# Output weights of two decode-attention problems in larger transfers: wo as 16 rows per partition

## The chip, the cores and the metric

The kernel runs on one core of one Trainium2 chip. The metric is the device time of one execution in microseconds (us). The times below are medians of several executions; the profile is of one execution.

## What is computed

Two independent problems, A and B, of the same shape are computed and their outputs are concatenated. Each is one step of decoding with a sliding window: 2 sequences, 1 query position, 32 query heads on 16 key and value heads, head size 128, a window of the last 4096 of 16384 cached positions, model width 576, all in bf16.

```
W = 4096; rep = 2
q = (x @ wq).reshape(B, Sq, Hq, Dh).transpose(0, 2, 1, 3)
k = repeat(k_cache[:, :, Sk - W:, :], rep, axis=1)
v = repeat(v_cache[:, :, Sk - W:, :], rep, axis=1)
p = softmax(einsum("bhqd,bhkd->bhqk", q, k) * Dh ** -0.5)
o = einsum("bhqk,bhkd->bhqd", p, v)
out = o.transpose(0, 2, 1, 3).reshape(B, Sq, Hq * Dh) @ wo      # wo: 4096 x 576
return concatenate([out_A, out_B], axis=-1)
```

## The kernel before

**Steps.** The work is cut into 16 steps, `ND` of them, 8 for A and 8 for B. A step is one slab of keys (4 MB: 4 pairs of sequence and key head, with 32 rows of each, 32 KB a partition) and the slab of values that belongs to it. Two steps make a group `G` of 8 query heads; there are 8 groups (`NG`), 4 in each problem (`GPP`). The slabs stream through a ring of 4 slots in SBUF (`ring`), all issued from the SP queue in one fixed order, `stream`: the two wq, then K0, K1, V0, K2, V1 and so on to K13, V12, K14, K15, V13, V14, V15. A slab's transfer waits until the slab four places before it has been read. V15, the last, comes in two pieces of 3 MB and 1 MB.

**One step.** For step `s` the vector engine (DVE) transposes the K slab in four parts (`do_X`, L494), and TensorE (PE) multiplies each with the spread-out queries `zq` (`do_S`, L519 and L170, into `st`). One step later come the maximum (`do_max`, L529), its transposition (`do_nm`, `do_nm2`, L542, L547), the exponential on ACT (`do_exp`, L564), the transposition of the result on DVE (`do_pC`, L572), and at the step's end the product with V (`do_PV`, L610, into `acc`), copied out by ACT (L622).

**One group.** GpSimd reduces the copied result (L629, L632, L637), `do_comb` turns it (L650), `do_norm` divides by the sums of the softmax (L674) and spreads the heads over 16 column positions (L683, `om`, with `maskD`). `do_redist` is two small matmuls with `maskS` (L710) that move the elements so that partition `p` holds what belongs to the rows of wo that lie on it; ACT copies this to `Rsb` (L730). `do_proj` then makes 8 pairs of matmuls, 512 and 64 columns wide, of `Rsb` with 8 rows of wo per partition (L757 and L170, into `ot` and a bank of `tb`). The sum over a problem's groups stays in `ot` for the 512 columns; the 64 are added up on DVE in `o_rest` (L773, L776). `do_E` finishes a problem.

**Order.** Each engine executes its instructions in the order in which this program adds them. A step's loop adds them over four parts `u`; the combine, norm and redistribute of group `G` stand in step `2G + 3`, and its projection at the end of that step, after the last `do_S` and ahead of `do_PV`:

```python
            do_S(s, NU - 1)
            if D2 >= 0 and D2 % 2 == 1 and s < ND - 1:
                do_proj(D2)
                if D2 == SPP - 1:
                    do_E(0)
```

with `D2 = s - 2`. So groups 0 to 5 are projected in steps 3, 5, 7, 9, 11 and 13. The add of the 64 columns is DVE's next instruction after `pC` and stands ahead of the next step's first transpose. Group 6 is projected in the tail after the last step, ahead of the two PV of V15; group 7, the last, in another form: its first step by a redistribution over 4 rows, its second by heads, from four last pieces of wo (L277 and L262) that are loaded behind V15.

**wo before.** `wob` has two buffers of 8 rows per partition. Group `G`'s 1152 KB of wo are one transfer (`issue_wo`, L275), ahead of K2, K4, K6, K8, K10, K12 and K14 in the stream; from group 2 on it waits for the projection of group `G - 2`.

Of the kernel before, what the change touches and what calls it, by code (L numbers as in the profile page):

```python
# [59 lines left out]
def build_kernel(nc, probs, out, cfg=None):  # L60
# [38 lines left out]
    PIECES = [(0, 96), (96, 128)]  # L99
    HEADS = [(0, 1), (2,), (3,)]  # L100
# [4 lines left out]

    es = ExitStack()
    with es:
# [3 lines left out]
        wqr = sb("wqr", [128, NPROB, HH], BF16)  # L111
        wob = sb("wob", [128, 2, 8, NOUT], BF16)
        xT = sb("xT", [128, NXC, NPROB, 128], BF16)
        maskP = sb("maskP", [128, 2], BF16)
        x_dup = sb("x_dup", [NPROB * Bb, DREM, 2], BF16)
        x_sb = sb("x_sb", [NPROB * Bb, D], BF16)
        ident_b = sb("ident_b", [128, 128], BF16)
        zq = sb("zq", [128, 4, NZQ, ZW], BF16)
        qrow = sb("qrow", [128, 1024], BF16)
        qtr = sb("qtr", [128, 1024], BF16)  # L120
# [5 lines left out]
        ones_b = sb("ones_b", [128, 128], BF16)  # L126
# [9 lines left out]
        oTg = sb("oTg", [128, 2, 16], BF16)  # L136
        om = sb("om", [128, 2, 256], BF16)
        Rsb = sb("Rsb", [128, 2, Bb, 8], BF16)
        maskS = sb("maskS", [128, 8], BF16)
        maskA = sb("maskA", [128, 4], BF16)  # L140
# [3 lines left out]
        mask4S = sb("mask4S", [128, 4], BF16)  # L144
# [3 lines left out]
        maskJ = sb("maskJ", [128, 4], BF16)  # L148
        ident_r = sb("ident_r", [128, 32], BF16)
        out_sb = sb("out_sb", [Bb, NPROB, NOUT], BF16)  # L150
# [57 lines left out]
        for G in range(NG):  # L208
            if not by_group(G):
                continue  # L210
            s_ = 2 * G + 2
            w_at.setdefault(("K", s_) if s_ < ND else ("V", s_ - LS), []).append(G)
# [11 lines left out]
        def issue_slab(n):  # L224
# [9 lines left out]
            if n == len(stream) - 1:  # L234
                for n_, (ja, jb) in enumerate(PIECES):
                    def fq(e, n_=n_, ja=ja, jb=jb):
                        return e.dma_start(ring[:, r, ja * 128:jb * 128], src[:, :, ja * 128:jb * 128]).then_inc(piece_sem[n_], 16)  # L237
                    pieces.append(dma_op("sp", piece_sem[n_], 1, fq, deps, "%s%d_q%d" % (kind, D_, n_)))
                issue_wo(NG - 1)
                return  # L240
# [16 lines left out]
        def issue_last(woP, pc, r0, deps):  # L257
            for n_, hs in enumerate(HEADS):
                def f(e, n_=n_, hs=hs):
                    t, r = divmod(hs[0], 2)  # L260
                    row = t * HH + r0 + 256 + 128 * r
                    return e.dma_start(wob[:, pc, 4 + hs[0]:4 + hs[0] + len(hs), :],  # L262
                                       woP[row:row + 128 * len(hs), :].rearrange("(h d) n -> d h n", d=128)).then_inc(wl_sem[n_], 16)
                wo_last.append(dma_op("sp", wl_sem[n_], 1, f, deps, "wl%d" % n_))

        def issue_wo(G):
            woP = probs[G // GPP][4]
            pc = G % 2
            r0 = (G % GPP) * 512
            deps = [proj[2 * (G - 2) + 1]] if G >= 2 else []  # L270

            def f(e):
                if by_group(G):
                    src = woP.rearrange("(t r) n -> t r n", t=2)[:, r0:r0 + 512, :].rearrange("t (p s) n -> p t (s n)", s=8)
                    return e.dma_start(wob[:, pc, :, :].rearrange("p s n -> p (s n)"), src).then_inc(wo_sem[pc], 16)  # L275
                src = woP.rearrange("(t r) n -> t r n", t=2)[:, r0:r0 + 256, :].rearrange("t (p s) n -> p t (s n)", s=4)
                last = e.dma_start(wob[:, pc, 0:4, :].rearrange("p s n -> p (s n)"), src).then_inc(wo_sem[pc], 16)  # L277
                return last
            wo_dma[G] = dma_op("sp", wo_sem[pc], 1, f, deps, "wo%d" % G)
            if not by_group(G):  # L280
                issue_last(woP, pc, r0, deps)

        def issue_until(n_needed):
            while nxt[0] <= n_needed:
                for G in w_at.pop(stream[nxt[0]], []):
                    issue_wo(G)
# [43 lines left out]
        def init_small():  # L330
# [5 lines left out]
                maskS[:], ident_b[:].rearrange("d (a s) -> d s a", s=8), AX.X, ALU.max), [p_ident_b], "maskS")  # L336
            init["mask4D"] = S.add("dve", lambda e: e.tensor_reduce(
# [325 lines left out]
        def do_norm(D_):  # L663
            G, sl = D_ // 2, D_ % 2
            n, bank = comb_at[D_]
            deps = [comb[D_], chain[(G, "rsb")]]
            if by_group(G):
                if G >= 2:
                    deps.append(spread[G - 2])

                def f_nm(e):
                    last = None
                    for l_ in range(2):
                        last = e.tensor_tensor(  # L674
                            oTg[:, G % 2, :].rearrange("d (b l r t) -> d l b t r", b=Bb, l=2, r=2)[:, l_],
# [4 lines left out]
                deps = [norm[D_], init["maskD"]]  # L680
                if G >= 2:
                    deps.append(redist[G - 2])
                spread[G] = S.add("dve", lambda e: e.tensor_tensor(  # L683
                    om[:, G % 2, :].rearrange("d (h k t) -> d h k t", h=8, t=2),
                    oTg[:, G % 2, :].rearrange("d (h t) -> d h t", t=2).unsqueeze(2).broadcast_to([128, 8, 16, 2]),
                    maskD[:].unsqueeze(1).unsqueeze(3).broadcast_to([128, 8, 16, 2]), ALU.mult), deps, "spread%d" % G)
                return
            dst = oTn[:, :, :].rearrange("d (t r) b -> d b t r", t=2) if sl else \
                oTg[:, G % 2, 0:8].rearrange("d (b r t) -> d b t r", b=Bb, r=2)
            if sl == 0:  # L690
                deps.append(spread[G - 2])
# [3 lines left out]
            if sl == 0:  # L695
                spread[G] = S.add("dve", lambda e: e.tensor_tensor(
                    om[:, G % 2, :].rearrange("d (h k t) -> d h k t", h=4, t=2),
                    oTg[:, G % 2, 0:8].rearrange("d (h t) -> d h t", t=2).unsqueeze(2).broadcast_to([128, 4, 32, 2]),
                    mask4D[:].unsqueeze(1).unsqueeze(3).broadcast_to([128, 4, 32, 2]), ALU.mult),
                    [norm[D_], init["mask4D"], redist[G - 2]], "spread%d" % G)  # L700
# [3 lines left out]
        def do_redist(G, idle=0):  # L704
            NS = 8 if by_group(G) else 4

            def fn(e, bank):
                last = None
                for b in range(Bb):
                    last = e.matmul(bank[:, NS * b:NS * b + NS], om[:, G % 2, 128 * b:128 * b + 128],  # L710
                                    maskS[:, :] if by_group(G) else mask4S[:, :], start=True, stop=True)
                return last
            last = [None]

            def fn_(e, bank):
                last[0] = fn(e, bank)
                return last[0]
            n, bank, op = tb_job(fn_, "redist%d" % G, [spread[G], init["maskS"], init["mask4S"]])
            if idle:
# [5 lines left out]
                S.add("pe", f_idle, [chain[(ND - 1, "exp")], init["maskB"]] + fin_ops, "idle%d" % G)  # L725
            redist[G] = op
            deps = [op, wo_dma[G]] if by_group(G) else [op]
            if G >= 2:
                deps.append(proj[2 * (G - 2) + 1])
            r_ev[G] = S.add("act", lambda e: e.activation(  # L730
                Rsb[:, G % 2, :, 0:NS], bank[:, 0:NS * Bb].rearrange("d (b s) -> d b s", b=Bb), ACTF.Copy), deps, "rev%d" % G)
            tb_consumer[n] = r_ev[G]
# [6 lines left out]
        def do_proj(D_):  # L739
            G = D_ // 2  # L740
            P = G // GPP
            pc = G % 2
            new = G % GPP == 0
            if by_group(G):
                parts = [([(Rsb[:, pc, :, s_], s_) for s_ in range(8)], [r_ev[G]], new, True, True)]
            elif D_ < ND - 1:
                parts = [([(Rsb[:, pc, :, s_], s_) for s_ in range(4)], [r_ev[G], wo_dma[G]] + fin_ops, False, False, False)]
# [3 lines left out]
            for lhs, deps, start, rstart, rstop in parts:  # L751
                def f(e, rest, lhs=lhs, start=start, rstart=rstart, rstop=rstop):
                    last = None
                    for n_, (l_, s_) in enumerate(lhs):
                        begin, end = n_ == 0, n_ == len(lhs) - 1
                        if by_group(G):
                            first = e.matmul(OT[0:Bb, 0:NB0], l_, wob[:, pc, s_, 0:NB0], start=start and begin, stop=end, skip_group_check=True)  # L757
                            last = matmul_again(e, first, rest[0:Bb, 0:NB1], wob[:, pc, s_, NB0:NOUT], rstart and begin, rstop and end)
                        else:
                            for half in range(2):  # L760
                                last = e.matmul(fin(half), l_, wob[:, pc, s_, half * NH:(half + 1) * NH],
# [28 lines left out]
        def do_E(P):  # L790
            G = (P + 1) * GPP - 1
            if G == NG - 1:
                e_ops[(P, 0)] = S.add("act", lambda e: e.activation(out_sb[:, P, 0:NH], fin(0), ACTF.Copy), [proj[2 * G + 1]], "Elo%d" % P)
                e_ops[(P, 1)] = S.add("dve", lambda e: e.tensor_copy(out_sb[:, P, NH:NOUT], fin(1)), [proj[2 * G + 1]], "Ehi%d" % P)
# [3 lines left out]
                out_sb[:, P, NB0:NOUT], o_rest[:, :], bank[0:Bb, 0:NB1], ALU.add), [proj[2 * G + 1], rest_add[G - 1]], "Ehi%d" % P)  # L798
            e_ops[(P, 0)] = S.add("act", lambda e: e.activation(out_sb[:, P, 0:NB0], OT[0:Bb, 0:NB0], ACTF.Copy), [proj[2 * G + 1]], "Elo%d" % P)

        def do_out(P, c0, c1, eng, deps):
            dma_op(eng, out_sem, 1, lambda e: e.dma_start(
                out[:, 0, P * NOUT + c0:P * NOUT + c1], out_sb[:, P, c0:c1]).then_inc(out_sem, 16), deps, "out%d_%d" % (P, c0))
# [13 lines left out]

        for s in range(ND):
            D2 = s - 2
            c = s - 1  # L820
            for u in range(NU):
# [21 lines left out]
                if D2 >= 0 and D2 % 2 == 1 and s < ND - 1:  # L843
# [3 lines left out]
                    elif u == 3:  # L847
                        do_redist(D2 // 2)
            do_S(s, NU - 1)
            if D2 >= 0 and D2 % 2 == 1 and s < ND - 1:  # L850
                do_proj(D2)
                if D2 == SPP - 1:
# [23 lines left out]
        do_redist(D_ // 2)  # L876
# [7 lines left out]
        do_redist(D_ // 2, 3)  # L884
# [107 lines left out]
```

## Time and profile before

| | |
|---|---|
| median of 3 executions | 363.21 us (363.21 to 363.26) |
| profiled execution | 363.24 us |
| its span, first to last instruction | 362.0 us |
| mean granted TensorE clock | 0.859 |
| moved by DMA | 153.27 MB, 423 GB/s over the span |
| busy: PE, DVE, ACT, GpSimd | 227.9, 202.0, 68.7, 35.4 us |
| DVE transposes of K (L494) | 64, mean 2285 ns, 145.4 us |
| chain that ended last | DMA 71%, DVE 15%, PE 9%, ACT 3% |
| transfers of wo by group (L275) | 7 of 1152 KB |

The rows of the timeline give the start and the duration in us, the engine, the line in the program, the operation, output and inputs with their shapes, a count, and in brackets how long the engine had been idle before and which instruction ended that. PEld is the loading of weights into TensorE, PE the matmuls themselves. In the view of waits the columns are the waiting engine and line, what released it, the sum of the waits in us, their number and the longest.

### The profile page before, as it was taken

To read this page: it belongs to the slowest core of one execution; us is meant where nothing else is said; L and a number is where in the kernel's file an instruction comes from. 1 tells how busy PE (TensorE), PEld (TensorE's weight loads), DVE (VectorE), ACT (ScalarE), POOL (GpSimd) and SP (SyncE) were. 2 spreads that over 40 slices of the span, in tenths; PEclk is the share of its full clock that TensorE was granted. 3 is DMA by queue.
4 is the path that set the end of the run, shared out by engine and by line. 5 is a ranking of instruction groups with operands and counts; after the bars stand their busy time and mean duration, and the time that the engine had idled before them with its cause. 6 is when DMAs were issued, how large, how long until landed. Compare 5 with 4: busy or idle time off the path is not lost.

```text
span 362.0 us, 2758 instructions
## 1 busy us (share of the span) xinstructions
PE 227.9 (63%) x1326; PEld 58.5 (16%) x953; DVE 202.0 (56%) x176; ACT 68.7 (19%) x153; POOL 35.4 (10%) x55
## 2 busy tenths in 40 slices
PE   0399195576966647384874727775672749657775
PEld 0010021112221202111221201111120112211121
DVE  3113599483818466291936648092844829179831
ACT  1036503020300303020110203102020203002131
POOL 1000000003100040004000040001300040110020
PEclk9999589787696969889688978869897896969999
DMA  8999999999999999999999999999999999999996
GB/s 348 420 449 406 453 389 446 438 431 432 439 415 445 424 427 440 420 442 427 405 455 427 431 433 424 435 435 427 426 434 431 438 422 431 435 427 442 418 421 251
DMA packets 7067, 153.27 MB, mean 423 GB/s; under 512 B 776, under 2 KB 1296, under 8 KB 1680
## 3 DMA queue, kind: packets, MB, share of 16 engines
q1 hardware_dynamic: 7052, 153.10, 98.8%
q8 instruction: 9, 0.15, 0.2%
q14 instruction: 2, 0.02, 0.0%
q10 hardware_dynamic: 4, 0.00, 0.0%
HBM read 153.10 MB, written 0.00 MB: 423 GB/s over the span
## 4 chain that ended last, share of the span: by engine, by line
DMA 71%; DVE 15%; PE 9%; ACT 3%; SPq 1%; issue 0%
DMA ring<-in_B_k_cache_dram 34%; DMA ring<-in_A_k_cache_dram 26%; DVE xt L494 13%; DMA wob<-in_B_wo_dram 8%; PE st L170 4%; PE st L519 4%; DMA x_sb<-in_B_x_dram 3%; ACT qrow L444 1%; DVE qtr L454 1%; ACT qk L462 1%; PE st L429 1%; DVE nM L542 1%; ACT qrow L449 1%; PE tb L532 0%; SPq L237 0%
## 5 line engine op out<-in xcount | busy, mean ns | idle before, releaser
L494 DVE STREAM_TRANSPOSE xt<-ring 128x2048 f32<-128x2048 f32 x64 | 145.4, 2285 | 76.0 <-DMA ring<-in_B_k_cache_dram 39.2
L519 PE MATMUL st<-xt,zq 128*128 128x512 bf16 x256 | 116.7, 456 | 111.1 <-DVE xt L494 84.8
L170 PE MATMUL st<-xt,zq 128*128 128x512 bf16 x256 | 115.5, 451 | 0.0
L519 PEld LDWEIGHTS st<-xt,zq 128*128 128x128 bf16 x256 | 28.1, 110 | 207.6 <-DVE xt L494 99.8
L610 PE MATMUL acc<-ring,pC 128*32 128x512 bf16 x512 | 34.9, 390 | 2.9 <-DMA ring<-in_B_v_cache_dram 2.9
L547 ACT ACTIVATE nMrep<-nM 1x128 f32<-1x128 f32 x16 | 4.9, 308 | 140.0 <-DVE nM L542 140.0
L622 ACT ACTIVATE acc_sb<-acc 128x512 bf16<-128x512 f32 x16 | 9.6, 597 | 84.2 <-PE acc L610 84.2
L572 DVE STREAM_TRANSPOSE pC<-pR 128x1024 bf16<-128x1024 bf16 x16 | 19.5, 1219 | 4.0 <-ACT pR L564 2.1
L529 DVE TENSOR_REDUCE m<-st 128x1 f32<-128x1024 f32 x16 | 19.0, 1190 | 1.3 <-PE st L170 1.3
L629 POOL TENSOR_TENSOR acc_sb<-acc_sb,maskJ 128x1024 bf16<-128x1024 bf16 (+1 forms) x8 | 13.4, 1680 | 60.7 <-ACT acc_sb L622 60.7
L481 POOL TENSOR_TENSOR zq<-qk,maskA 128x128 bf16<-128x128 bf16 x16 | 6.4, 401 | 126.6 <-PE st L170 104.8
L564 ACT ACTIVATE pR<-st,bias_sb 128x1024 bf16<-128x1024 f32 x16 | 17.8, 1115 | 0.5
L454 DVE STREAM_TRANSPOSE qtr<-qrow 128x512 f32<-128x512 f32 x8 | 5.7, 712 | 20.1 <-ACT qrow L444 12.8
L394 ACT ACTIVATE st<-maskB 128x1024 f32<-128x1024 bf16 x16 | 16.5, 1032 | 1.6 <-POOL rsel L579 0.4
L610 PEld LDWEIGHTS acc<-ring,pC 128*32 128x32 bf16 x512 | 13.1, 97 | 17.1 <-DMA ring<-in_B_v_cache_dram 3.8
L757 PE MATMUL ot<-wob,Rsb 128*2 128x512 bf16 x56 | 15.7, 398 | 0.2 <-ACT Rsb L730 0.2
L579 POOL TENSOR_TENSOR rsel<-maskS,rsum 128x16 f32<-128x16 bf16 x8 | 1.7, 218 | 123.5 <-ACT pR L564 123.5
L170 PE MATMUL tb<-wob,Rsb 128*2 128x64 bf16 x56 | 11.0, 197 | 0.0
L354 PE MATMUL tb<-ident_b,x_sb 4*128 4x16 bf16 x4 | 0.3, 182 | 14.6 <-DVE x_dup L359 14.6
L776 DVE TENSOR_TENSOR o_rest<-o_rest,tb 2x64 f32<-2x64 f32 x3 | 0.6, 208 | 13.8 <-PE tb L170 13.8
L632 POOL TENSOR_TENSOR acc_sb<-acc_sb 128x512 bf16<-128x512 bf16 (+1 forms) x8 | 8.2, 1030 | 0.6
L542 DVE TENSOR_REDUCE nM<-tb 1x8 f32<-1x128 f32 x16 | 4.4, 273 | 6.3 <-PE tb L532 6.2
(85 smaller groups left out, 109.4 us busy)
## 6 DMA issues: line engine op xcount, KB each, us to landing
ring<-in_A_k_cache_dram SPq DMA_DIRECT2D x8, 4096.0 KB, 30.7
ring<-in_A_v_cache_dram SPq DMA_DIRECT2D x8, 4096.0 KB, 32.6
ring<-in_B_k_cache_dram SPq DMA_DIRECT2D x8, 4096.0 KB, 30.7
ring<-in_B_v_cache_dram SPq DMA_DIRECT2D x7, 4096.0 KB, 32.4
wob<-in_A_wo_dram SPq DMA_DIRECT2D x4, 1152.0 KB, 33.8
ring<-in_A_wq_dram SPq DMA_DIRECT2D x1, 4096.0 KB, 12.8
ring<-in_B_wq_dram SPq DMA_DIRECT2D x1, 4096.0 KB, 22.6
wob<-in_B_wo_dram SPq DMA_DIRECT2D x3, 1152.0 KB, 33.5
```

The source lines that it names most:

```text
L170: return e.add_instruction(mybir.InstMatmult(name=nc.get_next_instruction_name(), engine=i.engine, ins=[e.lower_ap(rhs), i.ins[1]], outs=[ ...
L394: chain[(s, "fill")] = S.add("act", lambda e: e.activation(ST[s % 2][:, :].rearrange("k (h j) -> k h j", h=2), maskB[:].unsqueeze(1).broad ...
L454: chain[(G, "qtr")] = S.add("dve", lambda e: e.transpose(qtr[:].bitcast(FP32), qrow[:].bitcast(FP32)), evs, "qtr%d" % G)
L494: Xop[(s, u)] = S.add("dve", lambda e: e.transpose(xt[:, i % NKT, :].rearrange("k (j w) -> k j w", w=64), ring[:, n % NR, :].bitcast(FP32) ...
L519: first = last = e.matmul(bank, zq[:, p4, s % NZQ, w0:w0 + 128], mv, start=False, stop=stop, skip_group_check=True)
L529: chain[(s, "max")] = S.add("dve", lambda e: e.tensor_reduce(m1[:, 0:1], ST[s % 2][:, :], AX.X, ALU.max), d, "max%d" % s)
L564: chain[(s, "exp")] = S.add("act", lambda e: e.activation(pR[:, :], ST[s % 2][:, :], ACTF.Exp, bias=bias_sb[:, 0:1], scale=SCALE, accum_ou ...
L572: chain[(s, "pC")] = S.add("dve", lambda e: e.transpose(pC[:, s % NPT, :, :].rearrange("k j c -> k (j c)"), pR[:, :]), d, "pC%d" % s)
L610: last = e.matmul(ACC[32 * cb:32 * cb + 32, 0:512], pC[:, D_ % NPT, j0_:j0_ + 4, :].rearrange("k j c -> k (j c)"), ring[:, n % NR, j0_ * 1 ...
L622: acc_ev[D_] = S.add("act", lambda e: e.activation(acc_sb[:, D_ % 2, :], ACC[:, :], ACTF.Copy), d, "accev%d" % D_)
L629: t = S.add("pool", lambda e: e.tensor_tensor(v, v, maskJ[:].unsqueeze(1).unsqueeze(3).broadcast_to([128, l1 - l0, 4, 128]), ALU.mult), [a ...
L757: first = e.matmul(OT[0:Bb, 0:NB0], l_, wob[:, pc, s_, 0:NB0], start=start and begin, stop=end, skip_group_check=True)
```

## The change

wo is kept as 32 rows per partition in one buffer, `wob`, filled by five transfers in place of eight (the last by heads stay as they were). Parts 0 and 1 are A's whole wo: partition `p` holds 32 consecutive rows, 16 of them from each part, 18 KB in one run. Part 2 is B's first two groups as 16 rows per partition; part 3 is group 6 with 8 rows and part 4 the last group with 4. They stand in the stream ahead of K4, K6, V11, V12 and behind V15. Part 1 waits for the last copy of the queries, since the upper half of the buffer first holds what only the start needs (the remainder of wq, the query rows, x and its transposition, the identity). Parts 2, 3 and 4 wait for the projections of groups 1, 2 and 3.

Groups that share a layout make a unit: `UNITS` are groups 0 to 3, 4 and 5, 6, and 7. Norms of a unit collect in `oTg`; one spreading (4, 8 or 16 positions), one redistribution (32, 16 or 8 columns, with new masks) and one copy to `Rsb` serve the whole unit, in the step in which its last group's stood. The projections of groups 0 to 5, each as large as before, stand at the ends of steps 9 to 14. B's output reuses `pR`.

```diff
+    UNITS = [(0, 4), (4, 2), (6, 1), (7, 1)]
...
+    def wo_slot(G):
+        return {0: 0, 1: 8, 2: 16, 3: 24, 4: 0, 5: 8, 6: 16, 7: 24}[G]
...
-        wqr = sb("wqr", [128, NPROB, HH], BF16)
-        wob = sb("wob", [128, 2, 8, NOUT], BF16)
-        xT = sb("xT", [128, NXC, NPROB, 128], BF16)
+        wob = sb("wob", [128, NSW, NOUT], BF16)
...
+            a = wob[:, NSW // 2:NSW, :].rearrange("p s n -> p (s n)")[:, used[0]:used[0] + n]
...
+        wqr = early([NPROB, HH])
+        qrow = early([1024])
+        qtr = early([1024])
+        xT = early([NXC, NPROB, 128])
...
-        for G in range(NG):
-            if not by_group(G):
-                continue
-            s_ = 2 * G + 2
-            w_at.setdefault(("K", s_) if s_ < ND else ("V", s_ - LS), []).append(G)
+        for part, at in ((0, ("K", 4)), (1, ("K", 6)), (2, ("V", 11)), (3, ("V", 12))):
+            w_at.setdefault(at, []).append(part)
...
-        def issue_wo(G):
...
+        def issue_wo(part):
+            lo, n, r0, P, deps, Gs = (
+                (0, 16, 0, 0, [], (0, 1)),
+                (16, 16, 16, 0, [qkeep.get(NG - 1)], (2, 3)),
+                (0, 16, 0, 1, [proj.get(3)], (4, 5)),
+                (16, 8, 1024, 1, [proj.get(5)], (6,)),
+                (24, 4, 1536, 1, [proj.get(7)], (7,)))[part]
...
+                if part < 2:
+                    src = woP.rearrange("(t p s) n -> p t s n", t=2, s=2 * n)[:, :, r0:r0 + n, :].rearrange("p t s n -> p t (s n)")
+                else:
+                    src = woP.rearrange("(t r) n -> t r n", t=2)[:, r0:r0 + 64 * n, :].rearrange("t (p s) n -> p t (s n)", s=n)
+                return e.dma_start(wob[:, lo:lo + n, :].rearrange("p s n -> p (s n)"), src).then_inc(wo_sem[pc], 16)
...
+                if G < g0 + nG - 1:
+                    return
+                nk, mD = {4: (4, "maskA"), 2: (8, "mask16D"), 1: (16, "maskD")}[nG]
...
+            NS, mS = {4: (32, "mask32S"), 2: (16, "mask16S"), 1: (8, "maskS")}[nG] if by_group(g0) else (4, "mask4S")
...
-                parts = [([(Rsb[:, pc, :, s_], s_) for s_ in range(8)], [r_ev[G]], new, True, True)]
+                parts = [([(Rsb[u % 2][:, :, s0 + s_], s_) for s_ in range(8)], [r_ev[u], wo_dma[G]], new, True, True)]
...
+        redist_at = {2 * (g0 + n) - 1: u for u, (g0, n) in enumerate(UNITS)}
+        proj_at = {9: 0, 10: 1, 11: 2, 12: 3, 13: 4, 14: 5}
...
-                    elif u == 3:
-                        do_redist(D2 // 2)
+                    elif u == 3 and s - 2 in redist_at:
+                        do_redist(redist_at[s - 2])
             do_S(s, NU - 1)
-            if D2 >= 0 and D2 % 2 == 1 and s < ND - 1:
-                do_proj(D2)
-                if D2 == SPP - 1:
+            if s in proj_at:
+                do_proj(2 * proj_at[s] + 1)
+                if proj_at[s] == GPP - 1:
                     do_E(0)
```

## The prediction

> **What bounds the kernel now.** I read the page's slices and queues first, then what the DMA queue waits for, then VectorE (DVE) and TensorE (PE) in order of time at the end.
>
> ```profile
> DMA  8999999999999999999999999999999999999996
> ...
> q1 hardware_dynamic: 7052, 153.10, 98.8%
> ```
>
> The 16 DMA engines are busy from the second slice to the last. So the span of 362.0 us is about what moving 153 MB takes, and work of the engines counts only where it makes a transfer late or stands behind the last one.
>
> ```profile
> SPq L241 <- DVE xt L494: 183.0, 14, 15.0
> SPq L241 <- PE acc L610: 77.1, 13, 8.0
> ```
>
> The queue waits for free ring slots, yet a slab lands a median of 30.7 to 32.6 us after issue (page, part 6) and takes 9.72 us itself: some 21 us of transfers are always queued ahead of it. An engine may be late by up to that before the DMA starves.
>
> ```profile
> 295.95 2.31 DVE L494 STREAM_TRANSPOSE xt<-ring 128x2048 f32<-128x2048 f32 x1 [6.99 <-DMA ring<-in_B_k_cache_dram]
> ...
> 307.85 1.20 DVE L572 STREAM_TRANSPOSE pC<-pR 128x1024 bf16<-128x1024 bf16 x1
> 313.10 0.21 DVE L776 TENSOR_TENSOR o_rest<-o_rest,tb 2x64 f32<-2x64 f32 x1 [4.05 <-PE tb L170]
> 318.14 2.31 DVE L494 STREAM_TRANSPOSE xt<-ring 128x2048 f32<-128x2048 f32 x1 [4.83 <-DMA ring<-in_B_k_cache_dram]
> ...
> 329.02 1.25 DVE L572 STREAM_TRANSPOSE pC<-pR 128x1024 bf16<-128x1024 bf16 x1
> 330.19 2.27 DVE L494 STREAM_TRANSPOSE xt<-ring 128x2048 f32<-128x2048 f32 x1
> 332.38 1.19 DVE L529 TENSOR_REDUCE m<-st 128x1 f32<-128x1024 f32 x1
> ```
>
> These are DVE's steps 13, 14 and 15. In step 13 a projection is made: its add (L776) stands in DVE's order behind pC and ahead of the next step's first transpose, and DVE idles 4.05 us for PE. It costs nothing there, since K14 comes later still (4.83 us). Step 14 has no projection, and step 15 (330.19) begins without a wait for data: K15 is already there.
>
> ```profile
> 350.79 0.38 PE L757 MATMUL ot<-wob,Rsb 128*2 128x512 bf16 x1 [0.17 <-ACT Rsb L730]
> ...
> 354.62 1.48 PE L610 MATMUL acc<-ring,pC 128*32 128x512 bf16 x24 [1.71 <-DMA ring<-in_B_v_cache_dram]
> 357.10 0.62 PE L610 MATMUL acc<-ring,pC 128*32 128x512 bf16 x8 [1.00 <-DMA ring<-in_B_v_cache_dram]
> ```
>
> ```profile
> 359.63 0.08 PEld L761 LDWEIGHTS st<-wob,oTn 128*2 128x2 bf16 x2 [0.20 <-DMA wob<-in_B_wo_dram]
> 359.99 0.08 PEld L761 LDWEIGHTS st<-wob,oTn 128*2 128x2 bf16 x2 [0.27 <-DMA wob<-in_B_wo_dram]
> ```
>
> In the tail PE waits for the two pieces of the last V and the last two pieces of wo. The spare time of the engines against the DMA is therefore 1.71 + 1.00 + about 0.3 = 3.0 us. It can be a little more: an idle time is counted from the modelled end of a matmul, while back-to-back ones start before it (L757 and L170 pairs follow each other every 0.245 us though one takes 0.38), some 0.19 us at each of two joints: 3.4 us at most.
>
> **The transfers.** Three pairs of 1152 KB transfers become three of 2304 KB. DVE's waits price one: K12 to K13 (276.51 to 295.95, two slabs) is 19.44 us, so 9.72 a slab; K13 to K14 (22.19, two slabs and one wo) leaves 2.75 us for 1152 KB, or 2.8 by issue plus landing of wo6 (273.0 + 35.4) against V12 (272.4 + 33.2). A fixed part and a rate through both sizes give a fixed part of 0.02 to 0.08 us, so three merged pairs save 0.07 to 0.24 us. I take 0.15. The Trainium skill (DMA: Bandwidth & Descriptors, "Anatomy of one DMA — SWDGE (gpsimd) path") fits about 2.0 us of fixed cost to a transfer issued by GpSimd; if SP's paid the same, three fewer would save an estimated 6 us. The rows, with the next transfer already waiting in the queue, show at most 0.08.
>
> **The order of the stream.** By the new places K2 to V2 move up by one wo (2.75 us), K6 to V6 back by one, K10 to V10 up by one, K12 up by two (5.5 us), V12 back by one; the others, with V11, K13, K14 and all behind, stand after as many bytes as before. Part 1 waits for the last q copy, done by 36 us, when K2 was issued, far ahead of its place at K6. Part 2 waits on SP for the projection of group 1 (step 10) ahead of V11, which itself waits for the PV of step 10 that PE runs right after. Part 3 likewise in step 11. Queued behind are only V11, K13 and later, with some 21 us of transfers ahead: nothing. V12 lands at 308.4 in place of 305.6, before its PV (312.4).
>
> **Removed and small.** Four of the seven spread, redistribute and evacuate chains with maskS go (0.42 us DVE, 0.20 PE, 0.18 ACT each), all in steps where DVE later waits 3.5 us or more for a K slab: zero, and under 1 us in each such step if that wait were gone. The three new masks are 3 x 0.28 us on DVE near 3 us, before a wait of 10.31 us for x: zero. The Rsb copies grow from 16 columns to 64 and 32; an ACT copy of 128x64 took 0.23 us at 14.93 against 0.18, beside the same waits: zero.
>
> **The projections move.** Groups 0 to 5 were projected in steps 3, 5, 7, 9, 11, 13 and are in 9 to 14 now. Steps 3, 5 and 7 lose DVE's wait, ahead of a DMA wait: zero. Steps 10 and 12 gain it. Step 10 runs from K10, 2.75 us earlier (232.1); its 12.8 us (234.83 to 247.65) and 4.25 more end at 249.2, and K11 lands at 251.5. Step 12 starts at 271.0 and ends near 287.7 (12.5 and 4.25); K13 comes at 295.9. Both hidden; without that cover either would cost 4.25.
>
> Step 14 is the one without cover. Add to pC's start at 329.02 what step 13 shows from pC to the add (313.10 - 307.85 = 5.25) and the add's 0.21, and step 15's first transpose starts at 334.4 to 334.5 in place of 330.19: 4.25 us later. From there to the projection of group 6 at 350.79 I find the chain tight: DVE's four transposes, maximum, nM, pC (330.19 to 341.6, no idle row), S on PE, maximum (idle 0.87, for PE), exp on ACT, the accumulator's copy right behind exp (346.30), GpSimd's three steps (346.96 to 349.26), combine, norm, spread, redistribute. PV14's wait for its V (0.17) is beside this chain, which goes through GpSimd. So the projection of group 6 shifts by the whole 4.25, and the PVs of the last V behind it are late.
>
> **Sum.** 4.25 later, 0.15 off because K14 lands that much earlier, 3.0 to 3.4 of spare time used up: 0.7 to 1.1 us, and I take the middle, 0.9. On the profiled execution's 363.24 (span 362.0 and 1.24 around it) that is 364.14; its distance to the median of the runs, 363.21, is 0.03, so 364.1.
>
> **Rivals.** *The DMA still ends last* (0.18): the delay is smaller or some link of the chain has spare time I don't see; PE idles 2.71 us for DMA in the last 8 us, which speaks for it, the tight rows against. It decides if the spare time is 4.1 us, 0.7 above what I count. Then only the transfers count: 363.21 less 0.07 to 0.24, 363.0: within 0.2%.
>
> *The wait is of the long kind* (0.06). L776 and L797 waited 5.68 and 5.69 us at 189.28 and 231.09, when PE was at half clock; 1.6 us more lateness goes straight to the end: 365.7. Against it: from 318.0 to 334.5 the clock is 0.80 because step 14 begins slow, but after 324.8 its matmuls start 0.22 us apart, full speed, and from 334.5 on the view of stretches shows 1.00.
>
> *The new wait cools PE* (0.08). PE idles about 2.2 us between the projection and step 15's first S (334.4 to 336.6). Waits of 1.84 (289.02) and 2.12 us (309.11) left the matmuls at 0.22 us; after 5.41 (298.32) they ran 0.43 apart. At half speed S (1.9 us) takes 1.7 us longer, of which about 1.3 lie beside DVE's second transpose: 0.4 more, 364.5. The Trainium skill (TensorE: Matmul & The Clock Gate, "Part 1: The HAM clock gate") speaks for it if the wait fills enough of a free-running 3.4 us window, against it otherwise.
>
> *Faster* (0.06): larger runs save more than any row says, and a link has slack. It decides once the three merges save over 0.73 us, 0.24 us each, three times what the rows allow, with the tail's lateness hidden too: 362.3 at 0.3 each. The Trainium skill's fit of 2.0 us to a transfer (above) would end here. If the rows of 18 KB were cut into the old packets, the merges would save nothing and the end would be 0.15 later, 364.25; that is inside the forecast's own range.
>
> **How the numbers follow.** The forecast, a tail late by step 14's wait, has 0.62; its own range is 363.7 to 364.7. A measurement of this kernel can tell about 0.2%, 0.73 us, from no change, and the bounds of the sum straddle it: I put 0.42 of the 0.62 above and 0.20 below. Slower: 0.42 + 0.06 + 0.08 = 0.56. Same: 0.20 + 0.18 = 0.38. Faster: 0.06. The range leaves out the faster case, most of the long wait and the forecast's far end: 362.9 to 365.2.
>
> **What the changed profile would show.** If right: an L776-like add in step 14 at about 334.2 with 4.05 us idle for PE; DVE's next transpose right behind; the projection of group 6 near 355; PE's last L610 groups with no DMA wait; the last wo pieces landing near 359.8, before PE asks for them. Waits for K13 and K14 should stay at about 8 and 5 us. If PE still waits for the last V, the first rival holds; if the queue's time between K slabs changes by more than 0.1 us, my price of the transfers is wrong.

## The result and the profile after

The changed kernel takes 363.87 us in the median of 22 executions (363.05 to 364.88), the kernel before 363.13 (362.93 to 363.30): 0.74 us more, a ratio of 1.0020 with a 95% interval of 1.0013 to 1.0026. The interval lies wholly above 1, so the kernel is slower, by as good as exactly the 0.2% that the prediction took as the least that can be told from no change. It forecast 364.1.

The profiled execution took 363.15 us (span 361.9). That is one of the three fastest of the 22, so its end shows less than the median's loss; its steps show where the loss is made. The page's slices and queues, after:

```profile
DMA  8999999999999999999999999999999999999995
...
q1 hardware_dynamic: 6620, 153.10, 98.7%
```

The DMA engines are as busy as before, with 432 packets fewer. DVE in order of time, steps 13 to 15 (start, duration, engine, line, operation, and in brackets the idle time before it and what ended that):

```profile
306.97 1.20 DVE L599 STREAM_TRANSPOSE pC<-pR 128x1024 bf16<-128x1024 bf16 x1
313.87 0.21 DVE L808 COPY o_rest<-tb 2x64 f32<-2x64 f32 x1 [5.69 <-PE tb L188]
317.75 2.31 DVE L521 STREAM_TRANSPOSE xt<-ring 128x2048 f32<-128x2048 f32 x1 [3.67 <-DMA ring<-in_B_k_cache_dram]
...
328.12 1.21 DVE L599 STREAM_TRANSPOSE pC<-pR 128x1024 bf16<-128x1024 bf16 x1
333.39 0.21 DVE L811 TENSOR_TENSOR o_rest<-o_rest,tb 2x64 f32<-2x64 f32 x1 [4.06 <-PE tb L188]
333.53 2.29 DVE L521 STREAM_TRANSPOSE xt<-ring 128x2048 f32<-128x2048 f32 x1
```

The add that stands in step 14 now (333.39) makes DVE wait 4.06 us for PE, and step 15's first transpose comes behind it, at 333.53 in place of 330.19. PE in the tail:

```profile
354.17 0.38 PE L792 MATMUL ot<-wob,Rsb 128*2 128x512 bf16 x1 [0.17 <-ACT Rsb L763]
...
356.11 1.91 PE L637 MATMUL acc<-ring,pC 128*32 128x512 bf16 x26
...
359.48 0.66 PE L796 MATMUL st<-wob,oTn 128*2 128x288 bf16 x8
```

Group 6's projection starts 3.38 us later (354.17 against 350.79). Both PV of the last V follow it without a wait for DMA. The last projection (359.48) does not wait for a piece of wo either: the last transfer landed at 359.54, while it ran (issue 331.24 and 28.3 to landing). The rows of this tail show no wait for DMA.

### The profile page after: what moved, and what is told of

Read it like the earlier page. It is cut to its first block, busy times and chain, and to the rows that moved or that the text cites. A ratio compares the mean times of both kernels' runs of the same rounds, so it can differ in the third digit from the quotient of the medians.

```text
span 361.9 us, 2728 instructions
## 1 busy us (share of the span) xinstructions
PE 221.1 (61%) x1316; PEld 56.3 (16%) x945; DVE 200.7 (55%) x175; ACT 68.2 (19%) x149; POOL 35.3 (10%) x55
## 4 chain that ended last, share of the span: by engine, by line
DMA 64%; DVE 20%; PE 10%; ACT 3%; POOL 1%; issue 1%; SPq 0%
DMA ring<-in_B_k_cache_dram 33%; DMA ring<-in_A_k_cache_dram 27%; DVE xt L521 17%; PE st L188 4%; DMA wob<-in_B_x_dram 3%; PE st L546 3%; DVE m L556 1%; ACT wob L471 1%; DVE wob L481 1%; PE ot L792 1%; ACT qk L489 1%; DVE nM L569 1%; PE st L456 1%; PE acc L637 1%; ACT wob L476 1%
## 5 line engine op out<-in xcount | busy, mean ns | idle before, releaser
L546 PE MATMUL st<-xt,zq 128*128 128x512 bf16 x256 | 112.6, 440 | 120.4 <-DVE xt L521 95.4
L188 PE MATMUL st<-xt,zq 128*128 128x512 bf16 x256 | 111.7, 436 | 0.0
L546 PEld LDWEIGHTS st<-xt,zq 128*128 128x128 bf16 x256 | 27.2, 106 | 215.6 <-DVE xt L521 112.1
L637 PE MATMUL acc<-ring,pC 128*32 128x512 bf16 x512 | 32.8, 381 | 0.0
L656 POOL TENSOR_TENSOR acc_sb<-acc_sb,masks 128x1024 bf16<-128x1024 bf16 (+1 forms) x8 | 13.4, 1679 | 68.8 <-ACT acc_sb L649 68.8
L508 POOL TENSOR_TENSOR zq<-qk,masks 128x128 bf16<-128x128 bf16 x16 | 6.3, 398 | 119.6 <-PE st L188 98.6
L792 PE MATMUL ot<-wob,Rsb 128*2 128x512 bf16 x56 | 16.7, 416 | 0.2 <-ACT Rsb L763 0.2
L481 DVE STREAM_TRANSPOSE wob<-wob 128x512 f32<-128x512 f32 x8 | 5.7, 711 | 19.4 <-ACT wob L471 12.0
L606 POOL TENSOR_TENSOR rsel<-masks,rsum 128x16 f32<-128x16 bf16 x8 | 1.7, 216 | 125.9 <-ACT pR L591 125.9
L585 ACT ACTIVATE bias_sb<-tb 128x1 f32<-128x1 f32 x16 | 2.7, 171 | 26.7 <-PE tb L579 26.7
```

The source lines that it names most:

```text
L188: return e.add_instruction(mybir.InstMatmult(name=nc.get_next_instruction_name(), engine=i.engine, ins=[e.lower_ap(rhs), i.ins[1]], outs=[ ...
L481: chain[(G, "qtr")] = S.add("dve", lambda e: e.transpose(qtr[:].bitcast(FP32), qrow[:].bitcast(FP32)), evs, "qtr%d" % G)
L546: first = last = e.matmul(bank, zq[:, p4, s % NZQ, w0:w0 + 128], mv, start=False, stop=stop, skip_group_check=True)
L637: last = e.matmul(ACC[32 * cb:32 * cb + 32, 0:512], pC[:, D_ % NPT, j0_:j0_ + 4, :].rearrange("k j c -> k (j c)"), ring[:, n % NR, j0_ * 1 ...
L656: t = S.add("pool", lambda e: e.tensor_tensor(v, v, maskJ[:].unsqueeze(1).unsqueeze(3).broadcast_to([128, l1 - l0, 4, 128]), ALU.mult), [a ...
L792: first = e.matmul(OT[0:Bb, 0:NB0], l_, wob[:, w0 + s_, 0:NB0], start=start and begin, stop=end, skip_group_check=True)
```

## Experiments

The theory: one change of order, group 5's projection at the end of step 14, makes DVE stand still ahead of step 15, and the tail is late by that less its spare time. The rivals: the transfers (their size, their order, the shared buffer); PE's 2 us of extra work in that step, whatever DVE does; and a DMA that ends last however late the tail is. All times are medians; before, in the same two sets of runs, took 363.09 and 363.11.

**Both projections in step 13.**

```diff
-        proj_at = {..., 12: 3, 13: 4, 14: 5}
+        proj_at = {..., 12: (3,), 13: (4, 5)}
...
```

> The changed kernel with group 5's projection at the end of step 13, behind group 4's, in place of step 14. Theory (DVE's wait for that projection in step 14 makes the tail late): DVE idles about 6 us in step 13 (4.06 and 1.95 more), still ahead of K14; step 15's first transpose follows step 14's pC at once, near 329.3; PE waits for the last V again; 362.9 us (before less 0.07 to 0.24), all executions within 0.4. Rival (the transfers: their size, order or the shared buffer): nothing of that is changed, so 363.9 as in the changed kernel, with its spread of 363.05 to 364.88.

Measured: 363.04 us (362.80 to 363.24), ratio to before 0.9997 (0.9988 to 1.0006). DVE:

```profile
313.83 0.21 DVE L808 COPY o_rest<-tb 2x64 f32<-2x64 f32 x1 [5.69 <-PE tb L188]
315.79 0.21 DVE L811 TENSOR_TENSOR o_rest<-o_rest,tb 2x64 f32<-2x64 f32 x1 [1.75 <-PE tb L188]
317.71 2.31 DVE L521 STREAM_TRANSPOSE xt<-ring 128x2048 f32<-128x2048 f32 x1 [1.71 <-DMA ring<-in_B_k_cache_dram]
...
328.05 1.25 DVE L599 STREAM_TRANSPOSE pC<-pR 128x1024 bf16<-128x1024 bf16 x1
329.22 2.27 DVE L521 STREAM_TRANSPOSE xt<-ring 128x2048 f32<-128x2048 f32 x1
```

Two waits of 5.69 and 1.75 us in step 13 cost nothing, since DVE still waits 1.71 us for K14 behind them; step 15 follows pC at once. All that the change lost is back, with its transfers and buffer untouched. (The first wait was expected at 4.06: group 4's projection ran partly at half clock in this execution.) PE waits for the last V again, 1.86 and 1.01 us.

**The kernel before with that projection alone moved.**

```diff
-            if D2 >= 0 and D2 % 2 == 1 and s < ND - 1:
+            if D2 >= 0 and D2 % 2 == 1 and s < ND - 3:
                 do_proj(D2)
...
+            if s == ND - 2:
+                do_proj(D2 - 1)
```

> The kernel before with one thing moved: group 5's projection from the end of step 13 to the end of step 14. Theory: 0.7 to 1.1 over before, 364.0 us, and a spread of over 1 us between executions, as the changed kernel has. Rival (the transfers): no change, 363.1 us, executions within 0.4.

Measured: 363.99 us (363.65 to 365.04), ratio 1.0027 (1.0018 to 1.0036). The move alone does what the change does: 0.90 us over before, against 0.74, and the intervals overlap.

```profile
329.08 1.19 DVE L572 STREAM_TRANSPOSE pC<-pR 128x1024 bf16<-128x1024 bf16 x1
334.33 0.21 DVE L776 TENSOR_TENSOR o_rest<-o_rest,tb 2x64 f32<-2x64 f32 x1 [4.06 <-PE tb L170]
334.46 2.29 DVE L494 STREAM_TRANSPOSE xt<-ring 128x2048 f32<-128x2048 f32 x1
```

Here step 15 begins at 334.46, 4.27 us later than before; the prediction had 4.25. (Counted from K14's first transpose, which came at 318.41 and not 318.14, it is 4.00.) These two runs settle that it is the projection's place and not the transfers.

**The projection left in step 14, DVE's add later.**

```diff
+                            if G == 5:
+                                late.append(add_rest)
+                                continue
+                            add_rest()
...
                             do_rsb(c // 2 - 1)
+                        if s == ND - 1:
+                            late[0]()
```

> The changed kernel with the projection left in step 14, but DVE's add of its 64 columns put behind step 15's first transpose, the maximum and the reciprocal. Theory (it is DVE's standing still, not PE's work): the first transpose starts near 329.3; the reciprocal waits for PE until about 333.7, so nM of step 14 comes at about 336.3 in place of 339.2; 362.9 to 363.1 us with a spread under 0.5. Rival (the 2 us of PE work in step 14 are what is late): 363.9 as in the changed kernel. Rival (the transfers): 363.9.

Measured: 362.96 us (362.67 to 363.45), ratio 0.9997 (0.9989 to 1.0006). The spread of 0.78 us is more than the 0.5 expected.

```profile
329.98 2.26 DVE L521 STREAM_TRANSPOSE xt<-ring 128x2048 f32<-128x2048 f32 x1
332.17 1.17 DVE L556 TENSOR_REDUCE m<-st 128x1 f32<-128x1024 f32 x1
334.43 0.26 DVE L621 RECIPROCAL rsb<-tb 128x16 f32<-128x16 f32 x1 [1.08 <-PE tb L611]
```

With the same PE work in the same step, the loss is gone: DVE does its first transpose and the maximum while PE projects, and waits 1.08 us in place of 4.06. So it is the order on DVE, one add of 0.21 us ahead of a transpose that did not need it. PE's extra work does not vanish: step 15's third transpose still comes 1.20 us later after K14's first than before (19.05 against 17.85), and PE's first wait for the last V shrinks from 1.71 to 0.49 us. That much is hidden in the tail's spare time.

**The spare time of the tail, measured.** In the kernel before, step 15's first transpose is made twice, or three times.

```diff
+            for _ in range(1 if (s, u) == (ND - 1, 0) else 0):      # 2 in the second kernel
+                deps = deps + [S.add("dve", lambda e: e.transpose(...), deps, "again")]
             Xop[(s, u)] = S.add("dve", lambda e: e.transpose(
```

> The kernel before with step 15's first transpose on DVE made twice (the same data to the same place), so that all behind it is 2.3 us late. Theory (the tail has 3.0 to 3.4 us of spare time against the DMA, and lateness beyond it goes to the end one to one): hidden, 363.1 us; PE's waits for the pieces of the last V shrink from 2.7 in sum to about 0.5. If the spare time is smaller, the time is over 363.1 by what is missing.

> The same with the transpose made three times: 4.6 us late. Theory: 4.6 less 3.0 to 3.4 is 1.2 to 1.6 us, 364.3 to 364.7, and up to 0.4 more if PE has fallen to half clock in the longer wait; PE's waits for the last V are gone. Rival (the DMA ends last however late the tail is): 363.1.

Measured: 363.23 us (363.03 to 363.60), ratio 1.0002 (0.9993 to 1.0011), and 364.71 (364.11 to 365.74), ratio 1.0043 (1.0029 to 1.0057). PE's PV of the last V with one more and with two more:

```profile
354.51 1.48 PE L614 MATMUL acc<-ring,pC 128*32 128x512 bf16 x24
357.00 0.61 PE L614 MATMUL acc<-ring,pC 128*32 128x512 bf16 x8 [1.00 <-DMA ring<-in_B_v_cache_dram]
```

```profile
356.92 1.91 PE L614 MATMUL acc<-ring,pC 128*32 128x512 bf16 x26
```

With one more the time is that of before within the interval: the wait of 1.71 us is used up and that of 1.00 is left, more than the 0.5 expected in sum. With two more it is 1.60 us longer. The six executions of that kernel lie in two clusters, 364.11 to 364.29 and 365.14 to 365.74, and none near the median; only one of the first was profiled, and what makes the second is open. So the tail ends last once it is late enough, against the rival by which the DMA always does.

The spare time follows from three marks in the profiled executions: K14's first transpose, step 15's third transpose, and the end of the execution. The table counts the second and the third from the first, in us. Before, that is 335.99 less 318.14 and 363.24 less 318.14.

| profile | third transpose | later than before | end | later than before | difference |
|---|---|---|---|---|---|
| before | 17.85 | | 45.10 | | |
| add later (above) | 19.05 | 1.20 | 45.20 | 0.10 | 1.10 |
| one more transpose | 19.67 | 1.82 | 45.13 | 0.03 | 1.79 |
| changed kernel, first profile | 21.62 | 3.77 | 45.40 | 0.30 | 3.47 |
| PE kept warm (below) | 21.62 | 3.77 | 45.49 | 0.39 | 3.38 |
| projection alone moved | 21.89 | 4.04 | 45.62 | 0.52 | 3.52 |
| changed kernel, second profile (below) | 22.11 | 4.26 | 45.85 | 0.75 | 3.51 |
| two more transposes | 22.36 | 4.51 | 46.31 | 1.21 | 3.30 |

Up to 1.8 us of lateness hardly reach the end. From 3.8 us on, the difference stays at 3.3 to 3.5 us: that much is spare, and what is over it goes to the end about one to one. One more transpose made step 15 only 1.82 us later by these marks, and not 2.3.

**PE kept warm ahead of step 14.** 18 matmuls, whose output is not used, in PE's wait for K14.

```diff
+                if s == ND - 3:
+                    def f_warm(e):
+                        for _ in range(18):
+                            r = e.matmul(ACC[:, 0:512], om[:, 1, 0:128], maskB[:, :], start=True, stop=True)
...
```

> The changed kernel with 18 extra matmuls of 512 columns on PE, whose output is not used, between step 13 and step 14, in the gap in which PE waits for K14 (about 315.7 to 319.6). Theory (the spread of the changed kernel is the clock at which step 14's first S and projection run): step 14 starts at full clock in every execution, its pC at 328.2 or earlier; 363.1 to 363.4 us with a spread under 0.6. If the clock is not what spreads the executions: 363.9 with 363.05 to 364.88 as before.

Measured: 363.39 us (363.07 to 363.82), ratio 1.0005 (0.9996 to 1.0015). The median is about 0.5 us below the changed kernel's two (363.87 and 363.94), and the intervals of the ratios just overlap. The spread says less: 0.75 us over 11 executions, more than the 0.6 expected, against 1.83 over 22 and 0.90 over 11 of the changed kernel (next run). The table by stretches, over step 14's first S (the stretch and its length, then each engine's busy time and instructions in the header's order, the granted clock, the DMA share and GB/s):

```profile
core 0: us, PE busy (x) PEld busy (x) DVE busy (x) ACT busy (x) POOL busy (x), PEclk, DMA share, GB/s
318.00:324.00 6.00, 3.67 (x17) 0.95 (x10) 6.00 (x5) 0.31 (x1) 0.00 (x0) 1.00 0.99 426
```

PE is at full clock there (1.00), where in the changed kernel it was at 0.72 and 0.50 (the next run's rows). Step 15's first transpose comes at 333.49, as in the first profile of the changed kernel (333.53). So in this profile the extra matmuls take away the half clock in step 14's first S, and not the wait of 4.06 us, which is still there. That the clock in step 14 makes up the rest of the spread is not shown.

**The changed kernel once more.**

> The changed kernel itself, for a second profile and more executions. Theory (the clock at step 14): executions between 363.0 and 364.9; the profiled one is about 0.9 us later in step 14 than the first (nM of step 13 at 324.2 to 324.4 in place of 323.5) if its first S runs at half clock to 324.5, and ends later by as much; if it runs as the first did, about 363.2.

Measured: 363.94 us (363.52 to 364.42), ratio 1.0020 (1.0011 to 1.0029). The profiled execution took 363.52 us. Its stretches:

```profile
318.00:324.00 6.00, 3.96 (x10) 0.81 (x6) 5.42 (x4) 0.00 (x0) 0.00 (x0) 0.50 1.01 437
336.00:341.00 5.00, 3.27 (x15) 0.85 (x9) 5.00 (x6) 0.31 (x1) 0.00 (x0) 1.00 1.00 433
```

The first profile of the same kernel had:

```profile
318.00:324.00 6.00, 3.88 (x12) 0.81 (x7) 5.89 (x5) 0.19 (x1) 0.85 (x3) 0.72 1.00 431
336.00:341.00 5.00, 4.79 (x16) 0.95 (x8) 5.00 (x5) 0.31 (x1) 0.00 (x0) 0.66 1.00 433
```

Where step 14's first S ran at half clock throughout (0.50 against 0.72), step 13's nM came at 323.88 and not 323.50, step 15's first transpose at 333.94 and not 333.53, and the end 0.37 us later. The expected 0.9 was too much; it was measured against the kernel before, whose K14 came later too. The longest execution, 364.88, was not profiled. A projection partly at half clock in step 14, as step 13's was in the first profile (a wait of 5.69), would give 1.6 us more and fit it; that was not seen and stays open.

**The transfers alone.** The kernel with both projections in step 13, each of the three large transfers as two of 8 rows.

```diff
+                    for h in range(2):
+                        src = ...[:, :, r0 + 8 * h:r0 + 8 * h + 8, :].rearrange("p t s n -> p t (s n)")
+                        r = e.dma_start(wob[:, lo + 8 * h:lo + 8 * h + 8, :]...).then_inc(wo_sem[pc], 16)
```

> The changed kernel with groups 4 and 5 both projected in step 13, and each of the three transfers of 16 rows made as two of 8 rows, one behind the other, in the same place of the stream. Theory (a merge saves about 0.05 us, since the queue is never empty): 0.15 us over the same kernel with whole transfers, 363.2; the three pairs take 5.55 to 5.6 us of the queue in place of 5.50. Rival (2 us of fixed cost to a transfer): 6 us more, 369.

Measured: 363.12 us (363.01 to 363.69), ratio to before 1.0002 (0.9993 to 1.0010), 0.08 over the kernel with whole transfers: not to be told from nothing by time. From K12 to K13, two slabs and part 2, DVE's transposes, which both wait for DMA, are 24.94 us apart (270.78 to 295.72) with two transfers. With one they are 24.92 in the changed kernel (270.61 to 295.53) and 24.92 to 24.94 in the four other profiles with whole transfers. So this merge saves at most 0.02 us, less than the 0.05 expected; 2 us of fixed cost are excluded. The other two merges, read in the same way from K3 to K4 and from K5 to K6, take 24.92 to 25.10 us with one transfer and 24.99 and 25.00 with two: no saving above that scatter.

## Why the prediction was right, point by point

- **The bound.** The DMA queue is full throughout, and the work of the engines counts only behind the last transfers. Right: of all that was moved, only step 14 mattered, and with its projection taken out of it (both in step 13) the time is that of before.
- **Steps 10 and 12, the removed chains, the masks, the waits on SP.** Hidden, as reckoned: DVE waited 9.07 us for K13 and 3.67 for K14. K14's was put at 5; step 13's projection ran partly at half clock in the profiled execution (5.69 in place of 4.05). In the second profile it did not, and the wait for K14 was 4.88.
- **Step 14's wait.** Right in place and size: 4.06 us at the add. The lateness of step 15's first transpose, counted from K14's first, was 4.00 with the projection alone moved, and 3.73 and 4.22 in the two profiles of the changed kernel. The 3.73 belongs to the profile in which step 14 ran faster: from K14's first transpose to step 14's pC it took 10.37 us, with a granted clock of 0.72 over its first S, against 10.84 with 0.50. The term was taken as one number and varies with the clock.
- **The spare time.** 3.0 to 3.4 forecast, 3.3 to 3.5 measured: the upper end or a little over it. The rows give 3.0 alone. The 0.4 that the prediction allowed for matmuls that begin before the one ahead has ended fits, but no run shows that the rest lies there.
- **The transfers.** 0.15 forecast for three merges, from a fixed part of 0.02 to 0.08 us (its own price of 2.8 us gives 0.09 for the upper bound). By the rows one merge saved at most 0.02, which for three would be 0.06, and the other two nothing above their scatter of 0.2; the interval of the time can't tell.
- **The sum.** 0.9 forecast, 0.74 measured, 0.90 for the move alone. The mechanism held. What the forecast has too much fits the first two terms of the sum, both off to the same side: a lateness taken a little too large and a spare time taken a little too small. The term of the transfers, some 0.1 too large, pulls the other way by less.
- **The rival that the new wait cools PE.** It does, in some executions: in the first profile PE fell to half clock at 336.5, after a wait of 2.20 us. Its price was nothing and not 0.4: from step 15's first transpose to step 14's nM it is 5.68 us in that profile (333.53 to 339.21) and in the second (333.94 to 339.62), where PE stayed at full clock. DVE is at its second transpose until then. What the prediction left open, how much of a stretch the wait must fill, is in the last section.
- **The rival of the long wait.** Not seen: all four profiles with the projection and its add in step 14 show 4.06 us there, not 5.69. The longest execution was not profiled.
- **The rivals that the DMA still ends last, and that the transfers gain more.** Fallen: PE's waits for the last V are gone, and a split transfer costs next to nothing.

## What to carry to other kernels

Work that is moved to fill an even schedule needs a look at each step that receives it: ask which engine waits for its result, what stands behind that wait on the engine, and whether the next data come later anyway. Five of six places were covered here by a wait for DMA, and the sixth, just ahead of the tail, was not. Before work is moved away, try to move the small instruction that waits for it: an add of 0.21 us put three instructions later (behind a transpose, the maximum and the reciprocal) took back the whole loss. Idle time in the tail's rows can be read as an allowance, here 3.0 us by the rows and 3.3 to 3.5 by the runs; what exceeded it went to the end about one to one.

## What was not expected of the hardware

A wait of PE of 2.20 us was followed by half clock in one execution (PEclk 0.66 from 336 to 341 us) and by full clock in another (1.00) of the same kernel with the same wait. The granted clock changes in stretches that are multiples of 3.41 us (3.41, 6.83, 10.24, 13.65 and longer in the trace of before) and lie differently against the program in each execution. The stretch of 3.41 us that held most of the wait, in the first profile and in the second:

```profile
333.09:336.50 3.41, 1.21 (x8) 0.49 (x4) 3.11 (x3) 0.00 (x0) 0.00 (x0) 1.00 1.01 432
```

```profile
334.31:337.72 3.41, 1.43 (x7) 0.39 (x4) 3.41 (x4) 0.00 (x0) 0.00 (x0) 1.00 0.98 423
```

PE's matmuls fill 1.21 us of the first, a share of 0.36, and half clock follows; they fill 1.43 us of the second, 0.42, and the clock stays. The ten traces of this case have 714 such stretches at full clock. All 131 with PE busy for up to 0.41 of the stretch were followed by half clock; of 26 with 0.417 to 0.424, 22 were and 4 were not; none of the 557 with 0.43 or more was. From half clock (278 stretches) the way back needed more: with up to 0.790 the clock stayed at half, with 0.791 or more it was full next. PE need not be idle to lose its clock, then. These shares go by the modelled ends of the matmuls, and hold for this case's traces.

The kernel before spread over 0.4, 1.0 and 0.6 us in its three sets of 22, 32 and 29 executions. The kernels whose tail ends last spread over 1.8 and 0.9 us (the changed kernel, 22 and 11), 1.4 (the projection alone moved, 10) and 1.6 (two more transposes, 6). That the clock makes this difference is likely, since two profiles of the changed kernel ended 0.37 us apart with it; for the longest executions it is not shown.
